# Batch 0 of a fused attention and feed-forward kernel: first loads moved to casting transfers on GpSimd, and its matmuls regrouped

## The chip, the cores and the metric

The kernel runs on one core of a Trainium2 chip. The metric is the device time of one execution in microseconds (us); lower is better. The kernel before takes 288.11 us (median of 3 runs, 288.1 to 288.44).

## The reference

```python
def _attn_ref(q_l, k_l, v_l, q_g, k_g, v_g):      # 8 batches, 8 heads, 512 local + 32 global rows, head size 64
    k_all = np.concatenate([k_g, k_l], axis=2); v_all = np.concatenate([v_g, v_l], axis=2)
    out_g = np.matmul(sm(scale * np.matmul(q_g, k_all.transpose(0, 1, 3, 2))), v_all)
    s_ll = scale * np.matmul(q_l, k_l.transpose(0, 1, 3, 2))
    s_ll = np.where(np.abs(pos[:, None] - pos[None, :]) <= 32, s_ll, -1000000000.0)
    s_lg = scale * np.matmul(q_l, k_g.transpose(0, 1, 3, 2))
    out_l = np.matmul(sm(np.concatenate([s_lg, s_ll], axis=-1)), np.concatenate([v_g, v_l], axis=2))
    return np.concatenate([out_g, out_l], axis=2)
def _moe_ref(x, w_in, w_out):                       # 4352 rows of 512; w_in 512 x 2048
    h = x @ w_in
    return (h * (1.0 / (1.0 + np.exp(-1.702 * h)))) @ w_out
```

Each of 8 batches has 8 heads. 512 local rows see a band of 64 neighbours and 32 global rows; the global rows see everything. The heads of a row are joined, and a feed-forward layer (512 to 2048, a sigmoid GELU, back to 512) follows. Inputs and output are float32; the kernel computes in bfloat16 and adds up in float32.

## The kernel before

A batch is worked as two "quads" of four heads. In batch 0 the quads are `a` (quad 0) and `c` (quad 1), objects of class `Quad`. The order of every engine's instructions is the order of the calls (a manual schedule); each engine goes through its own list in order, and semaphores join the lists. What a call does in batch 0:

- `B` writes the mask into PSUM by matmuls of an identity with a bias (TensorE, array form 128 rows by 128 columns); `S` adds the local scores (form 32 by 128); `gk` and `K` are scores against the global keys (form 32 by 32), `K` writing the bank `kb`.
- `X` and `XK` are the exponentials on ScalarE (tiles `e` and `ek`).
- `ekU` (form 32 by 32) and `U` (form 128 by 32) add up, for unit 0, the softmax sums and, for units 1 and 2, the weighted values, in banks `ov`; `Gm` (form 128 by 32) does so for the global rows, `og`.
- `R` makes reciprocals of the sums on VectorE (two transposes and a reciprocal), `XL(h)` multiplies them into the values and writes `xL`, `eg` and `G` do the global rows.
- `Tk`, `Tq`, `transpose_g` transpose keys, queries and global rows on VectorE; `ext` copies global queries beside the local ones.
- `h_mm` and `h_step` are the first feed-forward matmuls (L615), on `xL` and `w_in_sb`; kc 0 and 1 of the contraction come from quad `a`, kc 2 and 3 from quad `c`. `o_mm` (L655) is the second feed-forward layer. `fill` and `zero` are matmuls that add zero or whose result is not used.

The first loads of batch 0 go as plain float32 transfers on the ScalarE and SyncE queues (L149, L150): keys and queries of quad 0, in halves, into the tile `early`. They are cast to bfloat16 by ScalarE (`cast_act`, three times) and VectorE (L791). Global queries and keys come by SyncE (`load_g32`) and are cast by VectorE (`cast_g32`, L140). Everything else comes by casting transfers from GpSimd's queue, float32 in memory to bfloat16 on the core. Their order there is: queries, then keys of quad 1 (`load(0, (1,))`, L81 and L82), global values `rvg` (L122, L123), and in `load_rest` the values of batch 0 (L249), the 8 transfers of `w_in_sb` (L259; the mask copies L225 are put before the last two), the 4 of `w_out_sb` (L262), with batch 1's queries, keys and values among and behind them. GpSimd's transfers use eight semaphores in turn, so that each waits until the eighth before it has landed.

PSUM has four rotating one-bank tiles (`pbank`) and two two-bank tiles (`spair`); a new tile waits for the readers of the old one.

From batch 1 on, quads are objects of class `Wide`; their keys must be there before `a.S(0)` of batch 1, which stands between the `o_mm` of batch 0.

Of the kernel before, what the change touches and what calls it, by code (L numbers as in the profile page):

```python
# [12 lines left out]
F32 = mybir.dt.float32  # L13
# [7 lines left out]
def kernel(  # L21
# [53 lines left out]
    def load(b, us=(0, 1), kq=True):  # L75
        if b not in loaded:
            loaded[b] = (ld.tile([128, 2, 16 * D], BF16, name="rk"),
                         ld.tile([128, 2, 16 * D], BF16, name="rq"))
        if kq:
            s = slice(us[0], us[-1] + 1)  # L80
            nc.gpsimd.dma_start(out=loaded[b][1][:, s], in_=qf[b][:, s])  # L81
            nc.gpsimd.dma_start(out=loaded[b][0][:, s], in_=kf[b][:, s])  # L82
# [5 lines left out]
    def v_view(b, n):  # L88
        return vtiles[b % 2][:, : 8 * n * (D + 2)].rearrange("p (u j c d) -> p u j c d", u=2, j=4, c=n)
# [22 lines left out]
    def on_act(out_, in_):  # L112
        nc.scalar.activation(out_, in_, AF.Copy)  # L113
# [7 lines left out]
    def load_turned(eng, out_, in_):  # L121
        eng.dma_start(out=out_[32:128], in_=in_[0:96])  # L122
        eng.dma_start(out=out_[0:32], in_=in_[96:128])  # L123
# [7 lines left out]

    def load_g32(name, src):
        t = g32[name] = consts.tile([128, 2, D], F32, name="g32%s" % name)
        if name == "v":
            load_turned(nc.sync, t, src[:, 0:2, :])
        else:
            nc.sync.dma_start(out=t, in_=src[:, 0:2, :])

    def cast_g32(name, t):
        nc.vector.tensor_copy(t[:, 0:2, :D], g32[name])  # L140

    load(0, kq=False)
    rk, rq = loaded[0]
    early = ld.tile([128, 4, TB], F32, name="early", bufs=1)
    k32, q32 = (early[:, 2 * i : 2 * i + 2].rearrange("p a b -> p (a b)") for i in range(2))
    halves = (slice(0, 8 * D), slice(8 * D, 16 * D))
    load_g32("q", qgf)
    for f in halves:
        nc.scalar.dma_start(out=k32[:, f], in_=kf[0][:, 0, f])  # L149
        nc.sync.dma_start(out=q32[:, f], in_=qf[0][:, 0, f])  # L150
    load_g32("k", kgf)


    warm0 = consts.tile([128, 128], BF16)
    nc.gpsimd.memset(warm0, 0.0)
    step = consts.tile([128, 289], BF16)
    nc.vector.memset(step, 1.0)
    ones32 = consts.tile([128, 32], BF16)
    nc.gpsimd.memset(ones32, 1.0)
    nc.gpsimd.memset(rvg[:, :, D:], 1.0)  # L160
    bd = consts.tile([128, 4, 32], BF16)
    nc.gpsimd.memset(bd, 0.0)
    for j in range(4):
        r = (j + 1) % 4
        nc.gpsimd.memset(bd[32 * r : 32 * r + 32, j, :], 1.0)
    for i in range(2):
        vtiles.append(consts.tile([128, 8 * 5 * (D + 2)], BF16, name="v%d" % i))
        nc.gpsimd.memset(v_view(i, 4 + i)[:, :, :, :, D:], 1.0)
    nc.gpsimd.affine_select(
        out=step, in_=step, pattern=[[1, 289]], compare_op=ALU.is_ge,  # L170
        fill=0.0, base=-97, channel_multiplier=-1,
    )
    w_in_sb = wts.tile([128, 4, NKC, d_ff // 4], BF16)
    w_out_sb = wts.tile([128, FC, d_model], BF16)
    w_in_r = moe_w_in.rearrange("(u p h) f -> u p h f", u=2, h=2)
    w_out_r = moe_w_out.rearrange("(g p e) m -> p g (e m)", p=128, e=2)

    warm = consts.tile([128, 512], BF16)
    nc.vector.memset(warm, 0.0)

    def fill(n, ps, start=False):
        for _ in range(n):
            nc.tensor.matmul(ps[:, :128], lhsT=warm0, rhs=warm0, start=start, stop=start, skip_group_check=True)

    fill(21, psP.tile([128, 512], F32, name="w", tag="p"), True)

    qtiles = []
    for i in range(4):
        qt = consts.tile([128, 24, 32], F32, name="q%d" % i)
        nc.vector.memset(qt[:, 0:4, :], 0.0)  # L190
        nc.vector.memset(qt[:, 20:24, :], 0.0)
        qtiles.append(qt)

    WIN = ((0, 10), (6, 12), (14, 12), (22, 10))
    mask = consts.tile([128, 2, MW], BF16)
# [31 lines left out]
    def mask_rest():  # L227
        nc.gpsimd.memset(mask, 1.0)
        nc.gpsimd.memset(mask_at(0, 248, 16, 12)[96:128, :, 0:4], 0.0)
        nc.gpsimd.memset(mask_at(1, 236, 16, 12)[96:128, :, 8:12], 0.0)  # L230

    mask_rest()
    load(0, (1,))
    load_turned(nc.gpsimd, rvg[:, 0:2, :D], vgf[:, 0:2])

    qgT = consts.tile([128, NQ, 40], F32)
    nc.vector.memset(qgT[:, :, 32:], 0.0)
    kgT = consts.tile([128, NQ, 32], F32)
    def transpose_g(lo, hi, names="qk"):
        for name, dst, s in (("q", qgT, rqg), ("k", kgT, rkg)):  # L240
            if name not in names:
                continue
            nc.vector.transpose(dst[:, lo:hi, :32], s[:, lo:hi].bitcast(F32))
# [7 lines left out]
    def load_rest():  # L251
        load_v2(0)
        n = d_ff // 4
        for part in range(4):
            if part == 3:
                for m in MASKS:
                    make_mask(m)
            for u in range(2):
                nc.gpsimd.dma_start(out=w_in_sb[:, part, 2 * u : 2 * u + 2],  # L259
                                    in_=w_in_r[u][:, :, part * n : part * n + n])  # L260
        for g4 in (1, 0, 2, 3):
            nc.gpsimd.dma_start(  # L262
                out=w_out_sb[:, 4 * g4 : 4 * g4 + 4, :].rearrange("p (g e) m -> p g (e m)", e=2),
                in_=w_out_r[:, 2 * g4 : 2 * g4 + 2, :])
# [14 lines left out]
    def pbank(name):  # L279
        return psP.tile([128, 512], F32, name=name, tag="p")  # L280


    def spair():
        return [psS.tile([128, 2, 512], F32, name="s4", tag="s%d" % i) for i in range(2)]

    def bank(pair, j):
        return pair[j // 2][:, j % 2, :]

    class Quad:
# [29 lines left out]
            self.Tk()  # L319
            self.Tq()  # L320

        def ext(self, cs=(0, 1, 2, 3)):
            for c in cs:
                (r0, nr), t0, n = WIN[c], (0, 20, 1, 20)[c], (4, 3, 3, 4)[c]
                nc.vector.tensor_copy(
                    self.qt[:, t0 : t0 + n, r0 : r0 + nr],
                    qgT[:, self.Q, : n * nr].rearrange("p (t r) -> p t r", t=n))

# [47 lines left out]
                                     rhs=rv[:, :, ee] if len(rv.shape) == 3 else rv[:, :, :, ee],  # L376
                                     start=(ee == 0), stop=(ee == 1), skip_group_check=True)

        def X(self, rnd):
            e = self.E[rnd]  # L380
            if len(self.ps) == 4:
                for j in range(4):
                    n = RW + 32 if j == 2 else RW
                    nc.scalar.activation(e[:, j, :n], self.ps[j][:, :n], AF.Exp, scale=scale)  # L384
                return
            for i in range(2):
                nc.scalar.activation(e[:, 2 * i : 2 * i + 2, :RW], self.ps[i][:, :, :RW], AF.Exp, scale=scale)  # L387

        def K(self, e=None):
            if e != 1:  # L390
                self.kb = pbank("kb")
            self.gk(self.kb, self.q[:, 4:20], e)


        def eg(self):
# [217 lines left out]
    def h_mm(i, fc, hp, kcs):  # L613
        for kc in kcs:
            nc.tensor.matmul(hp[:, : width(i)], lhsT=w_in_c[:, fc // 4, kc, fc % 4 // 2, :, fc % 2],  # L615
                             rhs=(xL[i] if i < B else xG)[:, kc, :],
                             start=(kc == 0), stop=(kc == NKC - 1))
# [1 line left out]
    def gelu(out_, in_):  # L619
        nc.scalar.activation(out_, in_, AF.Gelu_apprx_sigmoid)  # L620

    spot = consts.tile([128, 2], F32)
    nc.gpsimd.memset(spot, 0.0)

    spot_p = consts.tile([1, 2], BF16)

    def behind(x):
# [5 lines left out]
    def exp_table():  # L633
        nc.scalar.activation(spot[:, 0:1], spot[:, 1:2], AF.Exp)
# [143 lines left out]
        for _ in range(n):  # L778
            nc.tensor.matmul(ps, lhsT=warm[:, 0:128], rhs=warm, start=False, stop=False, skip_group_check=True)

    def cast_act(r, f32, hf):
        nc.scalar.activation(r[:, 0, halves[hf]], f32[:, halves[hf]], AF.Copy)

    cast_act(rk, k32, 0)
    cast_act(rq, q32, 0)
    cast_act(rq, q32, 1)
    cast_g32("q", rqg)
    transpose_g(0, 2, "q")
    a.ext((0, 1))
    a.Tk(0, 8)  # L790
    nc.vector.tensor_copy(rk[:, 0, halves[1]], k32[:, halves[1]])  # L791
    a.Tk(8, 16)
    a.Tq(0, 8)
    a.Tq(8, 16)
    a.ext((2, 3))
    cast_g32("k", rkg)
    transpose_g(0, 2, "k")
    load_rest()
    a.B(0)
    a.B(1, split=True)  # L800
    fill(8, a.bk[1][3])
    a.S(0, added=True, part=0)
    a.S(0, added=True, part=1)
    a.X(0)
    a.S(1, split=True, added=True)
    zero(2, a.bk[1][3])
    a.X(1)
    c.Tq()
    c.ext()
    c.Tk()  # L810
    c.B(0)
    a.K()
    a.XK()
# [7 lines left out]
    pt = spair()  # L821
    c.B(1, split=True, js=(2, 3), more=[bank(pt, 0)])
    c.S(1, split=True, added=True)
    c.X(1)
    a.ekU(1)
    a.U(1)
    a.XL(0)
    c.K()
    c.XK()
    a.ekU(2, bank(pt, 2))  # L830
    a.U(2)
    a.XL(1)
    a.Gm()
    gTs[0] = moe.tile([128, FC, TB], BF16, name="gT")
    pt = spair()
    c.U(0)
    c.ekU(0)
    c.R()
    c.ekU(1)
    c.U(1)  # L840
    c.ekU(2)
    c.U(2)
    c.eg()
    for fc in range(4):
        h_mm(0, fc, bank(pt, fc), (0, 1))
    c.XL(0)
    c.XL(1)
    for kc in (2, 3):
        for fc in range(4):
            h_mm(0, fc, bank(pt, fc), (kc,))  # L850
    a.G()
    c.Gm()
    gelu(gTs[0][:, 0:2, :], pt[0])
    gelu(gTs[0][:, 2:4, :], pt[1])
    c.G()
    for fc in range(4, FC):
        h_step(0, fc)
    def osteps(i, *sts):
# [336 lines left out]
```

## Time and profile before

| | |
|---|---|
| median of 3 runs | 288.11 us |
| the profiled execution's own time | 287.94 us |
| its span | 286.0 us (1.94 us lie outside) |
| TensorE matmul busy | 280.4 us (98%) |
| VectorE, ScalarE, GpSimd busy | 205.3, 184.5, 95.3 us |
| casting transfers (queue q0, software_dynamic) | 17.83 MB, 55.9% of 16 engines |
| granted TensorE clock | 1.00 |

The span runs from the first instruction to the last. Busy time is the union of an engine's instructions. A matmul's end is modelled and includes the way through the array, so that TensorE can look busy where its starts are far apart: starts are the better guide. "Landing" is the time from a transfer's issue until its semaphore is complete.

### The profile page before, as it was taken

How to read it: one execution, taken by the hardware profiler on the slowest of the kernel's cores; microseconds unless marked ns; L12 is line 12 of the kernel's file. 1: busy time of each engine (PE TensorE's matmuls, PEld its weight loads, DVE VectorE, ACT ScalarE, POOL GpSimd, SP SyncE). 2: the span in 40 equal slices, each digit the busy share in tenths (PEclk: the TensorE clock that was granted, in tenths of full speed). 3: DMA queues.
4: the chain of work that ended last, by engine and by line, in shares of the span. 5: the costliest groups of instructions: out<-in, count | busy, mean ns of one | idle time of the engine just before them, and what ended most of it. 6: DMA issues, size and time to landing. Idle time of an engine off the chain costs nothing.

```text
span 286.0 us, 8845 instructions
## 1 busy us (share of the span) xinstructions
PE 280.4 (98%) x3727; PEld 179.5 (63%) x3727; DVE 205.3 (72%) x494; ACT 184.5 (65%) x297; POOL 95.3 (33%) x142
## 2 busy tenths in 40 slices
PE   8999999999999999999999999999999999999995
PEld 7544445544554488646884488647874589448884
DVE  7771367787689898679867998679867697363452
ACT  4847657568678784778649774877658761874331
POOL 8984550855946003920086004800040000000001
PEclk9999999999999999999999999999999999999999
DMA  7999995999999801993059803940122003200213
GB/s 203 156 191 207 203 165 79 147 224 130 155 175 187 151 3 48 94 191 60 10 88 150 147 2 77 100 66 5 28 51 73 2 3 76 73 0 2 73 35 115
DMA packets 59351, 28.23 MB, mean 99 GB/s; under 512 B 47472, under 2 KB 49776, under 8 KB 59312
## 3 DMA queue, kind: packets, MB, share of 16 engines
q0 software_dynamic: 51760, 17.83, 55.9%
q1 hardware_dynamic: 7120, 9.18, 11.5%
q8 instruction: 29, 0.48, 0.7%
q10 hardware_dynamic: 432, 0.66, 0.7%
q14 instruction: 10, 0.08, 0.1%
HBM read 36.31 MB, written 8.91 MB: 158 GB/s over the span
## 4 chain that ended last, share of the span: by engine, by line
PE 93%; DVE 2%; ACT 2%; DMA 1%; issue 0%; SPq 0%; DVEq 0%
PE hp L615 38%; PE px L726 13%; PE py L726 9%; PE op L655 9%; PE x L726 6%; PE s L560 6%; PE ov L586 5%; PE s L615 2%; DMA early<-in_q_l_dram 1%; DVE xL L471 1%; ACT e L384 1%; PE og L597 1%; PE s L356 1%; PE s L339 1%; ACT e L387 1%; DVE rs L466 1%
## 5 line engine op out<-in xcount | busy, mean ns | idle before, releaser
L615 PE MATMUL hp<-xL,w_in_sb 128*128 128x512 bf16 x480 | 105.4, 379 | 0.1
L615 PEld LDWEIGHTS <-w_in_sb 128*128 128x128 bf16 x576 | 56.1, 98 | 60.0 <-issue 0.4
L620 ACT ACTIVATE gT<-hp 128x512 bf16<-128x512 f32 x120 | 69.8, 597 | 23.9 <-PE hp L615 22.4
L571 ACT ACTIVATE e<-s 128x1016 bf16<-128x1016 f32 (+1 forms) x56 | 53.3, 1002 | 20.3 <-PE s L560 20.2
L726 PEld LDWEIGHTS <-gs 128*128 128x128 bf16 x480 | 46.2, 98 | 6.7
L699 DVE TENSOR_TENSOR gs<-gT 128x512 bf16<-128x512 bf16 (+1 forms) x90 | 30.3, 364 | 17.7 <-ACT gT L620 17.2
L576 POOL TENSOR_TENSOR e<-e,mask 128x1760 bf16<-128x1760 bf16 x4 | 13.3, 3320 | 81.1 <-ACT e L571 81.1
L98 POOL DMA_DIRECT2D v<-in_v_l_dram x40 | 31.0, 777 | 14.9 <-PE og L597 3.9
L726 PE MATMUL py<-wsum,gs 128*128 128x256 bf16 x240 | 30.3, 273 | 0.0
L655 PE MATMUL op<-w_out_sb,gT 128*128 128x512 bf16 x128 | 29.5, 380 | 0.0
L576 DVE TENSOR_TENSOR e<-e,mask 128x1712 bf16<-128x1712 bf16 (+1 forms) x24 | 25.2, 1049 | 5.6 <-ACT e L571 5.6
L512 DVE STREAM_TRANSPOSE kT<-rk 128x512 f32<-128x512 f32 x14 | 14.6, 1045 | 14.9 <-DMA rk<-in_k_l_dram 14.9
L759 POOL DMA_DIRECT2D out_dram<-ob x2 | 1.2, 598 | 69.7 <-ACT ob L113 69.5
L655 PEld LDWEIGHTS <-gT 128*128 128x128 bf16 x128 | 11.8, 98 | 13.9
L726 PEld LDWEIGHTS <-gT 128*128 128x128 bf16 x192 | 18.0, 98 | 2.7
L726 PE MATMUL px<-w_out_sb,gT 128*128 128x256 bf16 x160 | 19.2, 273 | 0.0
L726 PE MATMUL px<-w_out_sb,gs 128*128 128x256 bf16 x160 | 19.1, 273 | 0.0
L471 DVE TENSOR_TENSOR xL<-ov,rs 128x512 bf16<-128x512 f32 x27 | 17.8, 685 | 0.7 <-PE ov L438 0.2
L696 DVE TENSOR_TENSOR gs<-gT 128x1024 bf16<-128x1024 bf16 (+1 forms) x30 | 17.4, 579 | 0.0
L560 PEld LDWEIGHTS <-kT 32*128 32x128 bf16 x672 | 12.6, 93 | 7.6 <-issue 6.7
L113 ACT ACTIVATE ob<-px 128x512 f32<-128x512 f32 x10 | 6.0, 598 | 15.2 <-DVE zz L748 15.2
L560 PE MATMUL s<-q,kT 32*128 32x160 bf16 (+1 forms) x448 | 14.9, 246 | 0.0
(150 smaller groups left out, 360.3 us busy)
## 6 DMA issues: line engine op xcount, KB each, us to landing
out_dram<-ob SPq DMA_DIRECT2D x128, 64.0 KB, 3.0
rq<-in_q_l_dram POOLq DMA_DIRECT2D x5, 512.0 KB, 8.0
rk<-in_k_l_dram POOLq DMA_DIRECT2D x5, 512.0 KB, 10.0
v<-in_v_l_dram POOLq DMA_DIRECT2D x24, 96.0 KB, 4.9
w_in_sb<-in_moe_w_in_dram POOLq DMA_DIRECT2D x8, 256.0 KB, 8.3
w_out_sb<-in_moe_w_out_dram POOLq DMA_DIRECT2D x4, 512.0 KB, 10.3
rq<-in_q_l_dram POOLq DMA_DIRECT2D x5, 256.0 KB, 8.5
rk<-in_k_l_dram POOLq DMA_DIRECT2D x5, 256.0 KB, 7.9
```

Source lines behind the costliest of these rows:

```text
L98: nc.gpsimd.dma_start(out=vt[0:n, hs, c, :D], in_=vs[FIRST[c] : FIRST[c] + n, hs])
L471: nc.vector.tensor_mul(self.x[:, 2 * self.u + h, :], self.st[1 + h], self.st["rs"])
L512: nc.vector.transpose(flat[:, 0:Sl].rearrange("p (r t) -> p t r", t=16), loaded[self.b][0][:, self.u].bitcast(F32))
L560: nc.tensor.matmul(bank(self.ps, j)[:, at : at + n], lhsT=self.k[p, KEYS[c] : KEYS[c] + 128, e], rhs=qs[p, :, :, e], start=(e == 0), stop= ...
L571: nc.scalar.activation(self.E[rnd][:, 2 * i : 2 * i + 2, :n], self.ps[i][:, :, :n], AF.Exp, scale=scale)
L576: eng.tensor_mul(e, e, mask[:, rnd : rnd + 1, :n].to_broadcast([128, 4, n]))
L615: nc.tensor.matmul(hp[:, : width(i)], lhsT=w_in_c[:, fc // 4, kc, fc % 4 // 2, :, fc % 2], rhs=(xL[i] if i < B else xG)[:, kc, :], start=( ...
L620: nc.scalar.activation(out_, in_, AF.Gelu_apprx_sigmoid)
L655: nc.tensor.matmul(op, lhsT=gTs[i][:, fc, tci * 128 : tci * 128 + 128], rhs=w_out_sb[:, fc, :], start=(first and fc == 4 * f4), stop=(fc = ...
L696: nc.vector.tensor_tensor(sums[i][2][:, g, :n], t[:, g, 0, :n], t[:, g, 1, :n], ALU.add)
L699: nc.vector.tensor_tensor(sums[i][k][:, g, : n // 2], x[:, g], y[:, g], op)
L726: nc.tensor.matmul(out_, lhsT=lv[:, g, tt * 128 : tt * 128 + 128], rhs=rv[:, g, :], start=(g == 0 and k in ((1, 3, 4, 6) if self.apart els ...
```

## The change

All of it concerns batch 0 and what stands before it.

- The four halves of quad 0's keys and queries are loaded by GpSimd's casting transfers straight into `rk` and `rq`: both halves of the keys are its first two instructions, then the `affine_select` that makes `step`, then both halves of the queries. The casts on ScalarE and VectorE are gone.
- GpSimd then issues the global keys (casting), quad 1's keys, quad 1's queries (keys ahead of queries now) and only then the small fills (`ones32`, `rvg`, `v`, `bd`) with `rvg`'s loads among them. `mask_rest` moves behind six of the `w_in_sb` loads.
- The global queries still come by SyncE; their cast and the first two `ext` copies are ScalarE's, after a call that loads the exponential's table. `warm0` and `spot` are VectorE's fills; the clearing of `q` for quads 2 and 3 comes after batch 0's attention.
- In quad 1 of batch 0 VectorE does keys, `ext`, queries instead of queries, `ext`, keys.
- `fill(8)` becomes `fill(2)`. `c.K` stands right behind `c.S(1)`, into a bank of the score pair, `c.XK` between the second and third `c.X(1)`; `a.ekU(2)` stands beside `a.ekU(1)`, the three `c.ekU` stand together ahead of the three `c.U`; `c.Gm` is put between the kc 1 and kc 2 matmuls of the first `h_mm`.

```diff
     for f in halves:
-        nc.scalar.dma_start(out=k32[:, f], in_=kf[0][:, 0, f])
-        nc.sync.dma_start(out=q32[:, f], in_=qf[0][:, 0, f])
-    load_g32("k", kgf)
+        nc.gpsimd.dma_start(out=rk[:, 0, f], in_=kf[0][:, 0, f])
...
+    nc.gpsimd.affine_select(
+        out=step, in_=step, pattern=[[1, 289]], compare_op=ALU.is_ge,
+        fill=0.0, base=-97, channel_multiplier=-1,
+    )
+    for f in halves:
+        nc.gpsimd.dma_start(out=rq[:, 0, f], in_=qf[0][:, 0, f])
+    load_g(0, 2, "k")
+    nc.gpsimd.dma_start(out=rk[:, 1], in_=kf[0][:, 1])
+    nc.gpsimd.dma_start(out=rq[:, 1], in_=qf[0][:, 1])
     ones32 = consts.tile([128, 32], BF16)
     nc.gpsimd.memset(ones32, 1.0)
     nc.gpsimd.memset(rvg[:, :, D:], 1.0)
+    load_turned(nc.gpsimd, rvg[:, 0:2, :D], vgf[:, 0:2])
...
-    mask_rest()
-    load(0, (1,))
-    load_turned(nc.gpsimd, rvg[:, 0:2, :D], vgf[:, 0:2])
...
             if part == 3:
+                mask_rest()
                 for m in MASKS:
...
-    cast_act(rk, k32, 0)
-    cast_act(rq, q32, 0)
-    cast_act(rq, q32, 1)
-    cast_g32("q", rqg)
+    exp_table()
+    on_act(rqg[:, 0:2, :D], g32["q"])
     transpose_g(0, 2, "q")
-    a.ext((0, 1))
+    a.ext((0, 1), on_act)
     a.Tk(0, 8)
-    nc.vector.tensor_copy(rk[:, 0, halves[1]], k32[:, halves[1]])
     a.Tk(8, 16)
...
-    cast_g32("k", rkg)
     transpose_g(0, 2, "k")
+    nc.vector.memset(warm, 0.0)
     load_rest()
     a.B(0)
     a.B(1, split=True)
-    fill(8, a.bk[1][3])
+    fill(2, a.bk[1][3])
...
+    c.Tk()
+    c.ext()
     c.Tq()
-    c.ext()
-    c.Tk()
...
-    c.X(1)
+    c.X(1, (0, 1))
+    c.K(bank(pt, 1))
+    c.XK()
+    c.X(1, (2, 3))
     a.ekU(1)
+    a.ekU(2, bank(pt, 2))
     a.U(1)
     a.XL(0)
-    c.K()
-    c.XK()
-    a.ekU(2, bank(pt, 2))
     a.U(2)
     a.XL(1)
     a.Gm()
     gTs[0] = moe.tile([128, FC, TB], BF16, name="gT")
+    c.ekU(0)
+    c.ekU(1)
+    c.ekU(2)
     pt = spair()
     c.U(0)
-    c.ekU(0)
     c.R()
-    c.ekU(1)
     c.U(1)
-    c.ekU(2)
     c.U(2)
     c.eg()
     for fc in range(4):
         h_mm(0, fc, bank(pt, fc), (0, 1))
+    c.Gm()
...
     a.G()
-    c.Gm()
...
     c.G()
+    clear_q(2, 3)
```

More of the change, by code (lines that the diff above doesn't have):

```diff
@@ L133, in load_g32 @@
         t = g32[name] = consts.tile([128, 2, D], F32, name="g32%s" % name)
[L134 to L140, printed above, removed]
+        nc.sync.dma_start(out=t, in_=src[:, 0:2, :])
     load(0, kq=False)
@@ L144 @@
     early = ld.tile([128, 4, TB], F32, name="early", bufs=1)
-    k32, q32 = (early[:, 2 * i : 2 * i + 2].rearrange("p a b -> p (a b)") for i in range(2))
     halves = (slice(0, 8 * D), slice(8 * D, 16 * D))
@@ L148 @@
     for f in halves:
-        nc.scalar.dma_start(out=k32[:, f], in_=kf[0][:, 0, f])
-        nc.sync.dma_start(out=q32[:, f], in_=qf[0][:, 0, f])
-    load_g32("k", kgf)
+        nc.gpsimd.dma_start(out=rk[:, 0, f], in_=kf[0][:, 0, f])
     warm0 = consts.tile([128, 128], BF16)
-    nc.gpsimd.memset(warm0, 0.0)
+    nc.vector.memset(warm0, 0.0)
     step = consts.tile([128, 289], BF16)
     nc.vector.memset(step, 1.0)
+    spot = consts.tile([128, 2], F32)
+    nc.vector.memset(spot, 0.0)
+    nc.gpsimd.affine_select(
[7 more added lines that the diff above has]
+    nc.gpsimd.dma_start(out=rq[:, 1], in_=qf[0][:, 1])
     ones32 = consts.tile([128, 32], BF16)
@@ L160 @@
     nc.gpsimd.memset(rvg[:, :, D:], 1.0)
+    load_turned(nc.gpsimd, rvg[:, 0:2, :D], vgf[:, 0:2])
+    for i in range(2):
+        vtiles.append(consts.tile([128, 8 * 5 * (D + 2)], BF16, name="v%d" % i))
+        nc.gpsimd.memset(v_view(i, 4 + i)[:, :, :, :, D:], 1.0)
     bd = consts.tile([128, 4, 32], BF16)
@@ L165 @@
         nc.gpsimd.memset(bd[32 * r : 32 * r + 32, j, :], 1.0)
[L166 to L172, printed above, removed]
     w_in_sb = wts.tile([128, 4, NKC, d_ff // 4], BF16)
@@ L178 @@
     warm = consts.tile([128, 512], BF16)
-    nc.vector.memset(warm, 0.0)
     def fill(n, ps, start=False):
@@ L185, with clear_q @@
     fill(21, psP.tile([128, 512], F32, name="w", tag="p"), True)
[L187 to L192, printed above, removed]
+    qtiles = [consts.tile([128, 24, 32], F32, name="q%d" % i) for i in range(4)]
+    def clear_q(*quads):
+        for i in quads:
+            nc.vector.memset(qtiles[i][:, 0:4, :], 0.0)
+            nc.vector.memset(qtiles[i][:, 20:24, :], 0.0)
+    clear_q(0, 1)
+    qgT = consts.tile([128, NQ, 40], F32)
+    nc.vector.memset(qgT[:, :, 32:], 0.0)
+    kgT = consts.tile([128, NQ, 32], F32)
     WIN = ((0, 10), (6, 12), (14, 12), (22, 10))
@@ L230, in mask_rest @@
         nc.gpsimd.memset(mask_at(1, 236, 16, 12)[96:128, :, 8:12], 0.0)
-    mask_rest()
-    load(0, (1,))
-    load_turned(nc.gpsimd, rvg[:, 0:2, :D], vgf[:, 0:2])
-    qgT = consts.tile([128, NQ, 40], F32)
-    nc.vector.memset(qgT[:, :, 32:], 0.0)
-    kgT = consts.tile([128, NQ, 32], F32)
     def transpose_g(lo, hi, names="qk"):
@@ L320, in T, with ext @@
             self.Tq()
-        def ext(self, cs=(0, 1, 2, 3)):
+        def ext(self, cs=(0, 1, 2, 3), copy=nc.vector.tensor_copy):
             for c in cs:
                 (r0, nr), t0, n = WIN[c], (0, 20, 1, 20)[c], (4, 3, 3, 4)[c]
-                nc.vector.tensor_copy(
+                copy(
                     self.qt[:, t0 : t0 + n, r0 : r0 + nr],
@@ L377, in gk, with X @@
                                      start=(ee == 0), stop=(ee == 1), skip_group_check=True)
-        def X(self, rnd):
+        def X(self, rnd, js=range(4)):
             e = self.E[rnd]
             if len(self.ps) == 4:
-                for j in range(4):
+                for j in js:
                     n = RW + 32 if j == 2 else RW
@@ L387, in X, with K @@
                 nc.scalar.activation(e[:, 2 * i : 2 * i + 2, :RW], self.ps[i][:, :, :RW], AF.Exp, scale=scale)
[L389 to L392, printed above, removed]
+        def K(self, kb=None):
+            self.kb = pbank("kb") if kb is None else kb
+            self.gk(self.kb, self.q[:, 4:20])
         def eg(self):
@@ L620, in gelu @@
         nc.scalar.activation(out_, in_, AF.Gelu_apprx_sigmoid)
-    spot = consts.tile([128, 2], F32)
-    nc.gpsimd.memset(spot, 0.0)
     spot_p = consts.tile([1, 2], BF16)
@@ L779, in zero @@
             nc.tensor.matmul(ps, lhsT=warm[:, 0:128], rhs=warm, start=False, stop=False, skip_group_check=True)
-    def cast_act(r, f32, hf):
-        nc.scalar.activation(r[:, 0, halves[hf]], f32[:, halves[hf]], AF.Copy)
-    cast_act(rk, k32, 0)
-    cast_act(rq, q32, 0)
-    cast_act(rq, q32, 1)
-    cast_g32("q", rqg)
+    exp_table()
+    on_act(rqg[:, 0:2, :D], g32["q"])
     transpose_g(0, 2, "q")
-    a.ext((0, 1))
+    a.ext((0, 1), on_act)
     a.Tk(0, 8)
-    nc.vector.tensor_copy(rk[:, 0, halves[1]], k32[:, halves[1]])
     a.Tk(8, 16)
```

## The prediction

> **What bounds the kernel now.** The page first: TensorE is busy 98% of the span and carries 93% of the chain that ended last, so a gain must let TensorE's dense stream begin sooner. Next, the chain in order of time for 0 to 60 us (start, length, what) shows where that stream begins:
>
> ```profile
> 1.34 4.16 DMA early<-in_q_l_dram
> ...
> 5.52 1.27 ACT rq L782 x2
> ...
> 6.81 0.46 DVE q L315
> ...
> 7.31 0.47 PE s L356 x16
> 7.78 1.65 ACT e L387 x2
> ...
> 11.13 0.64 PE s L356 x16
> ...
> 13.77 1.80 ACT e L384 x4
> 15.57 0.50 ACT ek L411
> ...
> 17.89 3.56 PE s L615 x16
> ```
>
> The head is a chain: query load, two casts, transpose, scores, then ScalarE's exponentials, until the first `h_mm` at 17.82 (17.89 on the chain). From 21.7 TensorE is the chain almost alone: what `h_mm` gains is gained at the end, if later loads keep up. So I went on to the timeline and asked for single transfers with their landings:
>
> ```profile
> 5.80 1.06 PE L183 MATMUL s<-warm 128*128 128x128 bf16 x8
> 10.01 1.05 DVE L311 STREAM_TRANSPOSE kT<-rk 128x512 f32<-128x512 f32 x1 [0.48 <-DMA rk<-in_k_l_dram]
> 32.85 1.04 DVE L512 STREAM_TRANSPOSE kT<-rk 128x512 f32<-128x512 f32 x1 [10.20 <-DMA rk<-in_k_l_dram]
> 37.30 0.53 PE L560 MATMUL s<-q,kT 32*128 32x160 bf16 x16
> ...
> L81 POOL DMA_DIRECT2D rq<-in_q_l_dram x1: 552/552/552, 50.6 to 50.6; - x1
> DMA to landing us min/median/max: 4.3/4.3/4.3
> ```
>
> Quad c's scores also wait for a load (second line). Batch 1's keys land just as VectorE takes them (third), 4.45 us ahead of their matmuls (fourth). The last two lines are a 256 KB casting load with few others under way.
>
> **Part 1, quad a's loads.** Removed: the three ScalarE casts (0.63 each; 1.27 on the chain) and VectorE's (0.40 for keys, 0.23 and 0.61 for global rows). Added: casting loads on one GpSimd queue. Its issues: a 128-partition load takes 0.54 to 0.71, so two key halves from 0.81 take 1.2, the `affine_select` 0.43, two query halves 1.2: the last query half is issued at 3.04. When does it land? Rows: 128 KB stores from GpSimd at the end land 2.0 to 2.1 after issue (no other load, no cast); 256 KB loads land after 4.3 (above) and 4.7 (rq at 3.57, while the float32 loads run). In a row, loads land 1.33 apart per 256 KB (`w_in_sb`: 15.66 to 22.33 for five more) or 1.72 (rq 8.26, rk 9.98). Taking 4.3 as a fixed 3.0 and 1.3 for the data, the last half lands at 3.04 + 3.65 = 6.7; by the store rows at 5.2. I take 6.3, nearer to the loads. Then `Tq` 0.45, 0.04 to TensorE, scores 0.47: `a.X(0)` starts at 7.26 instead of 7.78, a gain of 0.5 (0.1 to 0.9). TensorE itself allows no more: `B` runs 3.50 to 5.80 from start to start, two fills follow, and the first part of `a.S(0)` needs some 0.4.
>
> The Trainium skill ("DMA: Bandwidth & Descriptors", Latency and other measured facts) puts the first byte of a transfer from GpSimd at about 1 us and from SyncE or ScalarE at about 0.6: against this change, 0.4 us per first load. The trace agrees for the loads at best (2.9 for the first float32 half), and not for the stores (2.0 to 2.1 from GpSimd, 2.2 from SyncE and ScalarE); by the page alone the gain here would be about 0.1.
>
> **Part 2, quad c's loads.** Keys are issued at 0.81 + 2.4 + 0.43 + 0.71 (global keys) = 4.35, queries at 4.95; before, queries at 3.57 and keys at 4.27. The queue then holds 0.2 of global keys and two times 1.33 to 1.72: queries land at 6.3 + 0.2 + 2.7 = 9.2 to 9.95; with part 1's bounds 8.1 to 10.3. I take 9.7; before, the last of the two landed at 9.98. What follows the late one is now `Tq` (0.71) and not `Tk` (1.05). VectorE has done keys (landed about 8.3, 1.05) and copies (0.60) by 9.95, so `c.Tq` ends at 10.66 (before 11.06), and `c.X(0)`, 0.70 behind, starts at 11.4. ScalarE would be free at 7.26 + 3.85 = 11.11 (X(0) to XK took 7.76 to 11.61), so the load decides: `c.X(0)` gains 0.42 (0.05 to 0.75) on 11.82.
>
> **Part 3, fewer stretches.** From the end of `c.S(1)` to `h_mm` (13.66 to 17.82) TensorE changes its array form eight times; now four. A `U` followed by another form takes 0.42 (16.65 to 17.07), followed by its own 0.32 (15.00 to 15.32): 0.1 a change, four saved. It also waits 0.15 for `c.XK` before `ekU`; with `c.XK` ahead of the last two exponentials that goes. At most 0.55; at least 0, if ScalarE becomes the end: X(1) and XK take 2.3 to 2.4 from there, `c.U` needs another 0.9, 3.3 in all against TensorE's 3.6 to 3.76. I take 0.4. `c.R` now begins when `c.U(0)` ends; 1.7 and `eg` and `XL(0)` (0.8) put kc 2 about 2.0 behind `h_mm`'s start, just when eight matmuls (1.73) and the moved `c.Gm` (0.3) are through. No gain or loss.
>
> **Part 4, what is pushed back on GpSimd.** All small fills now stand behind the loads: values of batch 0 are issued at 8.2 (before 6.24), `w_in_sb` at 11.5 (9.49), its last two at 19.2 (16.09, `mask_rest` 1.12 added before them). If landings moved alike, `w_in_sb` would come at 17.6 for a need at 17.0: 0.6 lost. But landings were 6 to 12 us behind issue, against 2.0 unhurried: the queue's bytes set them, and those are the same. I charge 0 (0 to 0.6). `eg`'s `bd` and `ones32` are ready at 8.2, first used at 10.9.
>
> **Part 5, later loads.** Before, batch 1's scores could start at 36.02 (last `ext`), 1.28 ahead of TensorE. With 0.8 gained 0.5 is left; if the starved queue around 8 to 9 us delays batch 1's keys by over 0.5, TensorE waits. I charge 0.05 (0 to 0.5).
>
> **Hidden:** ScalarE's table load, cast and `ext` (some 2.2 us) lie before its first exponential at 7.3; `clear_q(2, 3)` (0.6) lies in VectorE's idle 10.2 before 32.85.
>
> Sum: 0.42 + 0.4 - 0.05, about 0.75. 287.94 - 0.75 = 287.19 for an execution like the profiled one, 0.17 below the median of runs; so **287.4**.
>
> **Rivals.**
> - *One queue is too slow (slower, 0.17).* In the trace two neighbouring loads (issued 50.65 and 51.19) land at 54.97 and 57.19: 2.2 per 256 KB, with stores beside them. At that pace a's keys land at 5.1, its queries at 7.35, c's keys at 9.8, its queries at 12.0, and `c.S(0)` starts at 12.76 instead of 11.12: 1.65 lost, 0.4 regained, 289.4. It costs from c's queries landing after 10.76, over 0.2% after 11.34. For it: seven loads on one queue where two hardware queues shared the work. Against: those stores are missing here.
> - *Nothing moves (0.24).* Landings as in the rows nearest in time (4.7, then 1.72 per 256 KB): a's queries 7.2, c's 10.85, `c.S(0)` at 11.6, 0.5 lost and 0.4 regained: 288.2. The same, if loads gain 0.42 but grouping nothing (the change then doesn't do what it says): 287.7.
> - *The array clock stays low (slower, 0.04).* The eight fills start 107 ns apart for 128 columns, `h_mm`'s 217 for 512: TensorE runs at half rate until about 6.7, though the page's granted clock says 1.00. Six fills less leave it idle 0.64 more just then. If half rate lasted to `h_mm`, part 3's 3.6 would double: about 291. Against it: 0.29 idle at 9.4 in the trace did no harm. The Trainium skill ("TensorE: Matmul & The Clock Gate", What's actually happening) says that one busy window of about 3.4 us opens the gate, with a phase of its own; the trace opened it 5.6 after the first matmul.
>
> **Numbers.** The forecast has 0.53, with a range of its own from 286.8 (gains 0.75 and 0.55) to 287.7; a rest of 0.02 is late loads of part 4. About 0.2%, 0.58 us, is what a measurement of this kernel can tell from no change. Faster by more needs under 287.53: nearly all of the forecast's weight, 0.52; within 0.2% 0.26; slower 0.22. The range runs from 286.8 to 289.0, into the slow-queue case.
>
> **What would show it.** `a.X(0)` at 7.1 to 7.5 and no ACT between load and transpose; `c.Tq` ending near 10.7 and released by VectorE or a landing under 10; `h_mm` at 17.0 to 17.2; no TensorE wait for `w_in_sb`; the S of batch 1 at about 36.5. Wrong, if c's queries land after 10.8, if fills and scores keep 107 ns per 128 columns after 7 us, or if `h_mm` starts early and TensorE waits at batch 1's scores.

## The result and the profile after

The changed kernel takes 290.75 us (median of 4 runs, 290.26 to 291.31) against 288.11: 1.0086 times the kernel before, 95% interval 1.0069 to 1.0102. It is slower, and the forecast was faster. The profiled execution took 290.69, with a span of 288.7 against 286.0.

The page's first line and its chain by engine, after. TensorE's share of the chain was 93% before; it lost ten points, mostly to GpSimd and transfers:

```profile
span 288.7 us, 8829 instructions
...
PE 83%; DMA 7%; POOL 5%; DVE 3%; issue 1%; ACT 0%; POOLq 0%; DVEq 0%
```

The chain in order of time, after (start, length, what). Where the kernel before had one load and then ScalarE and TensorE, a load of quad c's queries now ends at 12.95, then GpSimd's issues and batch 1's keys lead up to batch 1's scores:

```profile
1.34 1.25 POOL rk L142 x2
...
5.38 7.57 DMA rq<-in_q_l_dram
...
13.23 3.51 POOL w_in_sb L255 x5
...
23.51 13.01 DMA rk<-in_k_l_dram
...
39.73 0.64 PE s L555 x23
```

The timeline after, asked engine by engine (start, length, engine, what; in brackets the idle time before it and what ended it):

```profile
1.34 1.25 POOL L142 DMA_DIRECT2D rk<-in_k_l_dram  x2 [0.82 <-POOLq L1167]
...
6.30 0.30 PE L180 MATMUL s<-warm 128*128 128x128 bf16 x2
7.54 0.43 PE L352 MATMUL s<-q,kT 32*128 32x120 bf16 x16 [0.94 <-DVE q L311]
8.59 0.94 PE L352 MATMUL s<-q,kT 32*128 32x80 bf16 x32 [0.62 <-DVE q L311]
...
9.05 1.66 ACT L383 ACTIVATE e<-s 128x856 bf16<-128x856 f32 x2 [4.56 <-PE s L352]
...
11.49 1.04 DVE L307 STREAM_TRANSPOSE kT<-rk 128x512 f32<-128x512 f32 x1 [2.36 <-DMA rk<-in_k_l_dram]
12.97 0.71 DVE L311 STREAM_TRANSPOSE q<-rq 128x512 f32<-128x512 f32 x1 [0.18 <-DMA rq<-in_q_l_dram]
...
13.74 0.67 PE L352 MATMUL s<-q,kT 32*128 32x200 bf16 x16 [0.33 <-DVE q L311]
...
36.54 1.04 DVE L507 STREAM_TRANSPOSE kT<-rk 128x512 f32<-128x512 f32 x1 [12.01 <-DMA rk<-in_k_l_dram]
39.73 0.53 PE L555 MATMUL s<-q,kT 32*128 32x160 bf16 x16 [0.29 <-ACT q L113]
```

Behind the two fills that are left TensorE waits twice for the halves of quad a's queries, `a.X(0)` starts at 9.05 instead of 7.76 (7.78 in the chain), quad c's keys come at 11.47 instead of 9.99, its queries at 12.95 instead of 8.26, and batch 1's scores now wait 0.29 where they waited for nothing. The timeline before, for quad c's queries, `c.S(0)` and `h_mm`:

```profile
8.29 0.71 DVE L315 STREAM_TRANSPOSE q<-rq 128x512 f32<-128x512 f32 x1
...
11.12 0.66 PE L356 MATMUL s<-q,kT 32*128 32x200 bf16 x16
...
17.82 2.55 PE L615 MATMUL s<-xL,w_in_sb 128*128 128x512 bf16 x11
```

The stages between 6 and 13 us, after (window; length of the window, then busy time and count of TensorE, its weight loads, VectorE, ScalarE and GpSimd; then granted clock, DMA share, GB/s):

```profile
6.00:8.00 2.00, 1.03 (x22) 0.73 (x21) 0.45 (x1) 0.00 (x0) 1.88 (x9) 1.00 1.09 108
8.00:9.00 1.00, 0.41 (x24) 0.39 (x24) 0.90 (x5) 0.00 (x0) 0.93 (x3) 1.00 1.03 150
9.00:10.00 1.00, 1.00 (x29) 0.51 (x19) 0.14 (x3) 0.95 (x2) 1.00 (x3) 0.88 1.07 170
10.00:11.00 1.00, 1.00 (x7) 0.58 (x6) 0.00 (x0) 1.00 (x2) 1.00 (x2) 0.50 1.64 167
11.00:12.00 1.00, 1.00 (x10) 0.57 (x11) 0.51 (x1) 1.00 (x4) 0.79 (x2) 0.50 1.95 148
12.00:13.00 1.00, 1.00 (x10) 0.27 (x3) 0.82 (x6) 0.57 (x2) 0.47 (x1) 0.50 2.20 139
```

One of these stages before:

```profile
10.00:11.00 1.00, 1.00 (x14) 0.41 (x12) 0.99 (x2) 1.00 (x4) 0.94 (x3) 1.00 2.38 139
```

From 10 us on TensorE's granted clock is half after, and full before. So there are two suspects for quad c's late start, its load and the clock, and they lie in the same microseconds.

**How batch 0 adds up.** Four starts in each trace split the time: `a.X(0)`; from it to `c.S(0)`; from there to `h_mm`; from there to batch 1's first scores ("S1").

| kernel | `a.X(0)` | to `c.S(0)` | to `h_mm` | to S1 | lowest clock, 8 to 17 us | ratio to before (95%) |
|---|---|---|---|---|---|---|
| before | 7.76 | 3.36 | 6.70 | 19.48 | 1.00 | |
| after | 9.05 | 4.69 | 6.14 | 19.85 | 0.50 | 1.0086 (1.0069 to 1.0102) |
| e1, e12 regrouping alone | 7.80, 8.31 | 3.31, 3.31 | 6.14, 6.15 | 19.49, 19.48 | 1.00 | 0.9985 (0.9975 to 0.9996), 0.9968 (0.9956 to 0.998) |
| e2 loads alone | 9.00 | 4.06 | 6.71 | 19.48 | 1.00 | 1.0105 (1.0068 to 1.0142) |
| e3 longer fills | 9.02 | 4.24 | 6.15 | 19.88 | 1.00 | 1.0091 (1.0075 to 1.0106) |
| e4 masks later | 8.78 | 4.63 | 6.15 | 19.65 | 1.00 | 1.0069 (1.0057 to 1.0081) |
| e5 float32 loads for a | 10.27 | 5.38 | 6.57 | 19.48 | 0.50 | 1.0101 (1.008 to 1.0122) |
| e6 fills on VectorE | 9.09 | 4.16 | 6.14 | 19.69 | 1.00 | 1.0065 (1.0044 to 1.0086) |
| e7 global keys by SyncE | 9.17 | 4.22 | 6.15 | 19.49 | 0.50 | 1.0082 (1.006 to 1.0104) |
| e8 a's keys float32 | 8.17 | 3.31 | 6.14 | 19.61 | 1.00 | 0.9986 (0.9976 to 0.9997) |
| e9 e7 and e3 | 9.16 | 3.31 | 6.37 | 19.26 | 1.00 | 1.0047 (1.003 to 1.0063) |
| e10 e9, e4 and e6 | 9.26 | 3.31 | 6.38 | 19.26 | 1.00 | 1.004 (1.0021 to 1.0059) |
| e11 e10, a's queries float32 | 8.08 | 3.31 | 6.15 | 19.51 | 1.00 | 0.9995 (0.9984 to 1.0006) |

The times and the clock are from one profiled execution each; the ratio is from all runs, each against runs of the kernel before made beside it. For the change, `h_mm` is later by 1.29 + 1.33 - 0.56 = 2.06 (19.88 against 17.82), S1 by 0.37 more, and the end by 0.3 beyond that.

### The profile page after: what moved, and what is told of

The parts are those of the page before. It is cut to its first block, busy times and chain, and to the rows that moved or that the text cites. A ratio compares the mean times of both kernels' runs of the same rounds, so it can differ in the third digit from the quotient of the medians.

```text
span 288.7 us, 8829 instructions
## 1 busy us (share of the span) xinstructions
PE 280.5 (97%) x3721; PEld 179.4 (62%) x3721; DVE 203.2 (70%) x491; ACT 183.6 (64%) x298; POOL 97.8 (34%) x145
## 4 chain that ended last, share of the span: by engine, by line
PE 83%; DMA 7%; POOL 5%; DVE 3%; issue 1%; ACT 0%; POOLq 0%; DVEq 0%
PE hp L610 34%; PE px L718 13%; PE py L718 9%; PE op L647 7%; PE x L718 6%; PE s L555 6%; PE ov L581 5%; DMA rk<-in_k_l_dram 5%; DMA rq<-in_q_l_dram 3%; POOL w_in_sb L255 2%; PE s L610 1%; POOL mask L227 1%; DVE xL L466 1%; PE og L592 1%; DVE rs L461 0%
```

## The experiments

**e1, e12: the regrouping alone.** The kernel before with the new order of TensorE's work from `c.X(1)` on; its loads untouched.

```diff
-    c.X(1)
+    c.X(1, (0, 1))
+    c.K(bank(pt, 1))
+    c.XK()
+    c.X(1, (2, 3))
...
+    c.Gm()
     c.XL(0)
```

> All loads, casts, fills and masks as before; only the regrouping of batch 0's matmuls as changed (c.K behind c.S(1) in a score bank, c.XK between the c.X(1) halves, a.ekU(2) beside a.ekU(1), the three c.ekU together, c.Gm between kc 1 and kc 2). Late queue (the casting loads on one GpSimd queue land later and carry the whole loss): this is 0.2 to 0.5 us faster than before, 287.6 to 287.9, with h_mm at 17.3 to 17.6 instead of 17.82. Regrouping (the new order of matmuls itself costs): 288.7 or more. Low clock (TensorE's half rate carries the loss): like before or faster, since here TensorE has no longer waits for loads.

> The kernel of e1 (the kernel before with the regrouping alone) once more, beside e11 on the same chip. In e1 it took 287.5, with an interval that ended at 0.9996. Theory: the regrouping is worth 0.45 to 0.6; again 0.9975 to 0.9995 times the kernel before, h at 17.2 to 17.4. Rival: e1 was a lucky draw of the load landings; then 1.000 within 0.001.

Measured: 287.5 and, on another chip, 287.62 (before there: 288.38). Both intervals lie under 1; e12 gained more than the 0.9975 to 0.9995 that I expected. In the timeline of e1:

```profile
17.25 1.90 PE L614 MATMUL s<-xL,w_in_sb 128*128 128x512 bf16 x8
```

against 17.82 before; `c.S(0)` is at 11.11 against 11.12. The profiled execution of e12 drew late loads (the last query half at 6.68, 6.12 before; `a.X(0)` at 8.31, `h_mm` at 17.77), but the stretch from `c.S(0)` to `h_mm` is 6.15 in it too. In every kernel with the old order (before, e2) this stretch is 6.70 or 6.71, in the others at full clock 6.14 or 6.15, save for e9 and e10 (in both, `h_mm` waits 0.16 for VectorE's `sT`). The regrouping is worth 0.56, and alone it is faster than both kernels.

**e2: the loads alone.** The changed kernel with the old order of matmuls from `c.X(1)` on (the diff of e1 backwards).

> The complement: casting loads on GpSimd, order of loads, casts, fills and masks as changed; the matmuls of batch 0 in the order of before, except that c still does keys, ext, queries. Late queue: 290.9 to 291.3, the changed kernel's 290.75 plus what the regrouping saves (0.2 to 0.5), c's queries landing near 12.95 as in the changed kernel. Regrouping: 288 to 289.5. Low clock: near 290.75.

Measured: 290.55; the runs spread from 289.52 to 293.49, so the loads cost 2.0 to 4.1 by its interval. The time lies under the 290.9 to 291.3 of the late queue and near the figure of the low clock, so it cannot choose between them; the trace can. `h_mm` in e2:

```profile
19.77 0.61 PE L611 MATMUL s<-xL,w_in_sb 128*128 128x512 bf16 x2
```

The granted clock is 1.00 in every stage up to there: in this execution the loads make `h_mm` 1.95 later without any low clock. The clock was not always so: three of e2's six executions have a mean clock of 0.997 to 0.999 and took 289.52 to 290.24, the other three 0.993 or 0.994 and took 290.86 to 293.49. A half-clock stretch like the change's (3.4 us, see the last section) lowers the mean by 0.006.

**e3: the clock kept up.** Idle TensorE is filled with matmuls that add zero.

```diff
-    fill(2, a.bk[1][3])
+    fill(20, a.bk[1][3])
     a.S(0, added=True, part=0)
+    fill(12, a.bk[1][3])
```

> The changed kernel with fill(20) instead of fill(2) before a.S(0) and fill(12) between its two parts, so that TensorE has work while the queries are under way (idle from about 6.5 to 7.5 and 8.0 to 8.6 in the changed kernel). Low clock: the granted clock stays 1.00 from 9 to 13 us (0.50 in the changed kernel) and the time falls by 1 us or more, to 289.7 or less. Late queue: the clock may stay high, but c.S(0) still waits for c's queries (13.0), so the time moves by 0.3 us at most.

Measured: 290.63, no better. The same window as above, in e3:

```profile
10.00:11.00 1.00, 0.58 (x7) 0.44 (x6) 0.00 (x0) 1.00 (x3) 1.00 (x2) 1.00 1.27 126
```

The clock is full, TensorE idles instead, and `c.S(0)` waits for the load (queries at 12.47). `h_mm` came at 19.41, 0.47 before the change's. But the chain of e3 reaches S1 over batch 1's keys, which landed at 36.08 (36.52 in the change), so that S1 could not follow at the distance of 19.48 that it has before:

```profile
24.00 12.08 DMA rk<-in_k_l_dram
...
39.29 0.64 PE s L555 x23
```

**e4: the mask work behind the last two `w_in_sb` loads.**

```diff
-            if part == 3:
-                mask_rest()
-                for m in MASKS:
-                    make_mask(m)
...
+        mask_rest()
+        for m in MASKS:
+            make_mask(m)
```

> The changed kernel with GpSimd's mask fills and mask copies (3.5 us) moved behind the last two w_in_sb loads, so that these are issued at about 16.7 instead of 20.2; w_out_sb's issue stays where it was. Starved queue (the DMA engines run out of work from 20 to 24 us, 157 GB/s instead of 200, while GpSimd makes masks, so that batch 1's keys land at 36.5 and TensorE waits 0.3 there): batch 1's keys land 0.5 to 0.9 earlier, TensorE does not wait for a.S(0) of batch 1, 0.3 to 0.5 us faster, 290.3 to 290.5. Late queue alone: 290.75 within 0.2, for h_mm starts at 19.9 as before this edit.

Measured: 290.17, a little under my 290.3 to 290.5. Batch 1's keys landed at 35.39 instead of 36.52, and S1 came 0.2 sooner behind `h_mm`. The interval overlaps that of the change.

**e5: quad a's loads and the global keys as before, all else as changed.**

```diff
-        nc.gpsimd.dma_start(out=rk[:, 0, f], in_=kf[0][:, 0, f])
+        nc.scalar.dma_start(out=k32[:, f], in_=kf[0][:, 0, f])
+        nc.sync.dma_start(out=q32[:, f], in_=qf[0][:, 0, f])
+    load_g32("k", kgf)
```

> The changed kernel, but quad a's keys and queries and the global keys come again as float32 transfers on ScalarE's and SyncE's queues and are cast as before; GpSimd begins with the affine_select and then quad c's keys and queries, all else as changed. Late queue (what stands ahead of them in the one queue delays c's loads): c's queries land at 8 to 9.5 instead of 12.95, a.X(0) starts at 7.8 to 8.3, and the time is at or below the regrouping alone, 287.2 to 287.9. If instead the fills behind the loads or the order keys, queries carried the loss: 289 or more.

Measured: 291.23 (the profiled execution, 292.64, is its longest run), no gain at all; I had expected 287.2 to 287.9. With quad a off GpSimd's queue, quad c's loads went out at 1.78 and 2.48 and competed: the second query half landed at 8.52 (6.12 before), the global keys at 10.97 (6.33), quad c's queries at 10.67. The timeline of e5:

```profile
11.00 0.23 DVE L788 CAST rkg<-g32k 128x128 bf16<-128x128 f32 x1 [1.19 <-DMA g32k<-in_k_g_dram]
...
15.65 0.90 PE L352 MATMUL s<-q,kT 32*128 32x200 bf16 x16
```

TensorE ran at half clock from 7.2 to 17.4 in this execution, and the mean clock of all five (0.982 to 0.988) is low, so that the start at 15.65 and the time are not due to the loads alone. The landings do show the loads at work: the early issue of quad c's loads costs quad a what its own queues gave it. So the streams of different queues hold each other up. The Trainium skill ("DMA: Bandwidth & Descriptors", Issuing engines are not separate DMA queues) says that transfers of all issuing engines run on the same 16 and interleave, and the trace agrees.

**e6: GpSimd's small fills on VectorE** (`ones32`, `rvg`, `v`, `bd`: `nc.gpsimd.memset` becomes `nc.vector.memset`).

> The changed kernel with the small fills that stand between quad c's loads and the values' loads on GpSimd (ones32, rvg, v, bd) made by VectorE before it would wait. Disturbed queue (GpSimd's fills at 5.9 to 8.2 slow the transfers under way; packets of quad c's keys take up to 1.08 us there): c's queries land before 11.5 instead of 12.95 and the time falls by 1 us or more. Late queue: c's queries land at 12.5 to 13; only the values come 1 us sooner, and the time falls by 0 to 0.4.

Measured: 290.04. The second quad's queries landed at 12.43, half a microsecond earlier than in the change and as in e2 to e4 (12.27 to 12.62), which left these fills alone: the fills are not what holds the queue up.

**e7: the global keys by SyncE,** as float32 with a cast on VectorE, instead of on GpSimd's queue between quad a and quad c.

```diff
     load_g32("q", qgf)
+    load_g32("k", kgf)
...
-    load_g(0, 2, "k")
...
+    nc.vector.tensor_copy(rkg[:, 0:2, :D], g32["k"])
```

> The changed kernel with the global keys as a float32 transfer on SyncE's queue and a cast on VectorE (as before) instead of a casting transfer of 128-byte packets between quad a's queries and quad c's keys. Small packets (those 256 packets hold up quad c's loads): c's queries land 1 us or more earlier, near 11.5, and the time falls by 1 us. Late queue by bytes: 0.2 to 0.8 earlier (one issue of 0.7 less), time 0.2 to 0.8 lower, 290.0 to 290.5.

Measured: 290.77. Quad c's queries land at 10.87, 2.1 earlier, as the case of the small packets had it, but the time stays, where that case had 1 us less. Timeline, then windows, of e7:

```profile
10.90 0.71 DVE L311 STREAM_TRANSPOSE q<-rq 128x512 f32<-128x512 f32 x1
...
13.39 0.67 PE L352 MATMUL s<-q,kT 32*128 32x200 bf16 x16
```

```profile
6.00:8.00 2.00, 0.63 (x14) 0.46 (x16) 0.54 (x2) 0.00 (x0) 1.81 (x9) 1.00 1.16 190
...
10.00:11.00 1.00, 1.00 (x5) 0.47 (x4) 1.00 (x6) 1.00 (x3) 1.00 (x2) 0.50 2.10 139
```

The queries are transposed by 11.61, and their scores begin 1.78 later: TensorE, at half clock, is still at the work ahead of them. Between 6 and 8 us the transfers move 190 GB/s here and 108 in the change.

**e8: a split,** on top of the regrouping: quad a's keys as float32 by ScalarE and SyncE, its queries first on GpSimd's queue, quad c's loads next, the mask work as in e4.

```diff
-        nc.scalar.dma_start(out=k32[:, f], in_=kf[0][:, 0, f])
-        nc.sync.dma_start(out=q32[:, f], in_=qf[0][:, 0, f])
+        (nc.scalar if f is halves[0] else nc.sync).dma_start(out=k32[:, f], in_=kf[0][:, 0, f])
+        nc.gpsimd.dma_start(out=rq[:, 0, f], in_=qf[0][:, 0, f])
...
-    cast_act(rq, q32, 0)
-    cast_act(rq, q32, 1)
```

> The regrouped matmuls of e1, with quad a's first loads split: keys as float32 halves, one on ScalarE's and one on SyncE's queue, with casts as before; queries as casting transfers, the first two of GpSimd, without ScalarE's casts; then affine_select, quad c's loads, the small fills, the rest, masks behind the last w_in_sb load. Late queue: queries land at 5.2 to 6.2, a.X(0) starts at 6.9 to 7.4 (7.8 in e1), c's loads land at 8.5 to 9.5, time 286.9 to 287.6, at or below e1. If one queue less is enough to delay: a.X(0) later than 7.8 and more than 287.7.

Measured: 287.81, as e1, not better. The query halves, GpSimd's first two instructions, landed at 6.10 and 7.06, 4.8 and 5.0 behind their issue, and `a.X(0)` began at 8.17, where I had expected 6.9 to 7.4: no sooner than with two float32 loads and two casts (7.76 before, 7.80 in e1, 8.31 in e12). That is the rival's case.

**e9: e7 and e3 together.**

> The changed kernel with two edits together: the global keys come over SyncE as f32 with a cast (as in e7), and the longer fills of e3 (20 ahead of a's first scores, 12 between the parts). Alone they moved the time to 290.77 and 290.63, against 290.75 for the change. Theory: two limits stand near one another in batch 0, the late second quad's queries (12.95 in the change) and the array's half clock between 10 and 13 us; taking away one leaves the other. Then both together give a granted clock of 1.00, the second quad's queries at about 10.9, its first scores at 11.7 to 11.9, batch 0's output matmul h at 17.9 to 18.2 instead of 19.88, and, with batch 1 then held by its keys, 288.4 to 289.3. Rival: one of the two counts for nothing and the loss is somewhere further on; then 290.3 to 290.8 again.

Measured: 1.0047 of before (median 290.12, 288.95 to 290.4). I had expected 288.4 to 289.3. The profiled execution is the shortest, 1.2 under the median, so what the others lose besides is not seen. In it, from `a.X(0)` to `c.S(0)` it takes 3.31, as in e1: that excess, 1.33 against before, is gone with both causes taken away, and was cut only to 4.22 and 4.24 with one. My numbers for `c.S(0)` and `h_mm` were missed (12.47, not 11.9; 18.84, not 18.2): I had forgotten that `a.X(0)` was itself 1.4 late. The chain of e9:

```profile
4.00 2.50 PE s L335 x16
6.51 1.12 PE s L180 x20
...
9.18 1.65 ACT e L383 x2
10.83 0.04 issue
10.87 0.63 PE s L335 x6
11.50 0.56 PE kb L371 x8
12.06 0.48 PE s L335 x4
12.54 0.60 PE s L352 x16
```

From the exponentials on there is no load and no gap in it. Up to them it runs over the added fills, so these have a part in the late `a.X(0)`.

**e10: e9 with e4 and e6.**

> e9 with the two edits on the later loads added: the mask work behind the last two input weight loads (e4) and the small fills of ones, values and block diagonals on VectorE (e6). Theory: with batch 0 mended, what is left is batch 1's keys, whose landing these two edits bring forward (e4 by 1.1 us, e6 by 0.7); the time comes to 287.8 to 288.5, that is to the kernel before or a little below it. Rival: the later loads are hidden; then this is e9 within 0.2 us. If the cause lies outside the loads and the clock, 289.5 or above.

Measured: 1.004 of before (median 289.28); its interval overlaps e9's. Its batch 0 is e9's, and so is its distance to S1. With batch 0 as late as it is here, mending the later loads shows no further gain; the forecast for it was missed. In its profiled execution (289.76) S1 is at 38.21, 0.11 behind e9's, and the span ends 1.03 behind: some 0.9 is lost behind S1, for a reason that stays open.

**e11: e10 with quad a's queries by the float32 queues,** cast on ScalarE, its keys still on GpSimd's queue.

```diff
+    for f, eng in zip(halves, (nc.sync, nc.scalar)):
+        eng.dma_start(out=q32[:, f], in_=qf[0][:, 0, f])
     load_g32("q", qgf)
...
-    for f in halves:
-        nc.gpsimd.dma_start(out=rq[:, 0, f], in_=qf[0][:, 0, f])
...
-    fill(20, a.bk[1][3])
+    fill(8, a.bk[1][3])
...
-    fill(12, a.bk[1][3])
```

> e10 with the first quad's queries taken off GpSimd's queue again: two float32 halves at the head of SyncE's and ScalarE's queues, both cast on ScalarE, its keys still casting loads on GpSimd; the fills are 8 and 0 instead of 20 and 12. In e10 the second quad's queries landed at 10.75, and its first scores still began only at 12.57, because the first quad's exponentials began at 9.28 (7.78 in the kernel before). Theory: what is left of the loss in e10 (h at 18.95 against 17.82) is the first quad's query halves behind its keys and the affine_select on GpSimd's queue (7.87 in e10). Then the halves land by 4.6, the exponentials begin at 6.9 to 7.4, the second quad's first scores at 10.3 to 11.0, h at 16.7 to 17.4, and the time is 286.8 to 287.8, a little below the kernel before. Rival: the two kinds of queue hold each other up as in e5; then the halves or the keys land after 6.5, the exponentials begin at 8 or later and the time is 288.5 or above. Third: with fewer fills the granted clock falls to 0.50 again, h at 19 or later.

Measured: 0.9995 of before (288.37), so the loss is gone; the gain hoped for is not there. The regrouping alone took 287.62 on the same chip (e12), so these loads still cost about 0.75. The query halves landed at 4.00 and 4.18 as expected, but the key halves at 5.77 and 6.67 (5.52 for the later one in e10), as the rival had it. The chain of e11:

```profile
2.04 4.63 DMA rk<-in_k_l_dram
...
6.70 0.61 DVE kT L307
...
7.36 0.74 PE s L352 x25
8.10 1.65 ACT e L383 x2
```

The last half to land, now one of the keys, sets `a.X(0)` again. Against e10 some 0.4 of the gain is due to the fills: there the second part of the scores stood behind the twelve (queries transposed by 8.34, scores at 8.80).

## Why the prediction was wrong, step by step

- **Part 1, quad a's loads** (gain 0.5 forecast, 1.29 lost): the term that failed is the landing of the last query half, "I take 6.3". It was 8.07, and the rest of the sum held: transpose, scores and `a.X(0)` follow within 0.98 (0.96 forecast). GpSimd's first transfer began at 1.34, not 0.81 (SyncE's began at 0.82 in the same trace), so the half was issued at 3.60 instead of 3.04; and it took 4.47 to land, where I had taken 3.26. I had split the 4.3 of a 256 KB load into a fixed 3.0 and 1.3 for data, and halved the second. The transfers' landings, after:

```profile
L155 POOL DMA_DIRECT2D rq<-in_q_l_dram x2: 560/568/576, 3.0 to 3.6; - x2
L158 POOL DMA_DIRECT2D rq<-in_q_l_dram x1: 571/571/571, 5.4 to 5.4; - x1
...
DMA to landing us min/median/max: 4.0/4.5/7.6
```

  A half (first line, 3.97 and 4.47) takes nearly as long as the whole 256 KB did before (4.3, 4.7). My bound of 6.7 was short as well. Before, the chain went on from the first query half, landed at 5.50, since the second landed at 6.12, while ScalarE cast the first. So the load that starts it is 2.57 later, the two casts saved are 1.27, and the difference of 1.30 is the loss. That the queries' place in the queue carries about 1.0 of the loss is shown by e11, where `a.X(0)` is back at 8.08 (e11 differs in other edits too).
- **Part 2, quad c's loads** (gain 0.42 forecast): quad c's queries landed 3.25 behind my 9.7. Of this 1.77 is part 1's error, handed on, and the other 1.48 belongs to this part: "0.2 of global keys" was the second mis-sized term. With them out of the queue (e7, e9) quad c's keys come 1.34 and 1.48 behind quad a's last half, and its queries 1.34 and 1.35 after them: the 1.33 to 1.72 of the prediction. With them in the queue quad c's keys came 3.21 behind the global keys' landing at 8.26. Taking them out brought quad c's queries forward by 2.1; at most 0.75 of that is the issue taken off GpSimd, and how the rest splits between the transfer's packets and what they do to the next one was not tried.
- **Part 3, fewer stretches** (0.4, at most 0.55): right, 0.56 (e1, e12, and by e2 in reverse). How it splits between the saved changes of form and the wait of 0.15 was not tried.
- **Part 4, what is pushed back on GpSimd** (0): the weights were in time; no TensorE wait for `w_in_sb` appears. **Part 5, later loads** (0.05, up to 0.5): 0.37 between `h_mm` and S1 in the profile after, with 0.29 of it the wait shown above. The chain after shows the link: GpSimd's issues stand behind the landing of quad c's queries at 12.95, and batch 1's keys behind these issues. So that late load delays S1 a second time; in e7, where it landed at 10.87, the keys landed at 34.26 and S1 followed `h_mm` by 19.49. That moving the masks (e4) recovers a measurable part of the time is not shown.
- **The rivals.** "One queue is too slow" came nearest: it had quad c's queries at 12.0 and `c.S(0)` at 12.76; 12.95 and 13.74 came, and 290.75 instead of its 289.4. Late landings were right, but that the numbers are near is partly luck. It gave all loads one pace of 2.2 per 256 KB; measured were 2.74 from quad a's keys to its queries, 3.40 to quad c's keys and 1.48 to its queries. A late start, a long landing and one small transfer did it. "The array clock stays low" happened too, from 10 to 13 us, and not by missing the first opening but by closing again. It is not what makes the change slow: of the change's four executions three have a mean clock of 0.993 or 0.994, and the fourth, at 0.998, took 290.80, in the midst of their 290.26 to 291.31. e3, at full clock, was no faster either, and the profiled executions of e2, e4 and e6 were slow without it. What it costs on top is open: in e2 the executions with the lower clock were the longer ones, in e4 they were the shortest and the longest. With the load mended and the clock not, it took the load's place in the trace of e7, and with both mended the excess is gone in that of e9. By their times e9 (1.0030 to 1.0063) is clear of e3 (1.0075 to 1.0106), but not of e7 (1.0060 to 1.0104), whose one execution at 0.998 took 290.63, as long as the rest.
- **The chances.** I gave 0.22 to slower; no case had quad a's queries later than 7.35. All cases let GpSimd's first load begin at 0.81 and took their landings from rows of 256 KB loads, and so shared their errors. The first sign of being wrong that the prediction names, c's queries landing after 10.8, is the one that came.

## What to carry to other kernels

When first loads change queues, cost them by when their issue begins and by the landing of a whole transfer behind it; halving a transfer here did not halve its landing. Work that needs four loads is set by the one that lands last: compare the landing that starts the chain, old and new (5.50 and 8.07), before counting saved casts (1.27). Where two edits each move little, look whether the two waits they remove lie in the same microseconds, and remove both (e3, e7, e9); and split the path into stretches, so that a gain (6.70 to 6.14) can be seen under a larger loss.

## What the runs showed of the hardware

- The granted clock of the change fell to 0.50 between 9 and 10 us (0.88 in that window), after TensorE had been busy 1.03 of 2.00 us (6 to 8) and 0.41 of 1.00 (8 to 9), with no single wait over 0.94. The Trainium skill ("TensorE: Matmul & The Clock Gate", What's actually happening) closes the gate after an idle window of about 3.4 us. The trace does not show a window of that length without work: TensorE was idle 1.6 of those 3 us.
- The clock records kept with the traces tell more. Full clock begins at 6.35 in the change and ends 3.41 later; half clock then lasts 3.41, and three times that in e5. TensorE's busy time in the first 3.41 of full clock was 1.85 in the change, 1.66 in e7 and 1.25 in e5, where the clock then fell, and 2.05 (e11) to 3.41 (e3) in the eleven other profiled executions, where it did not. In these traces the limit lies between 1.85 and 2.05 of 3.41; no run was made to test it. Of the two rows at the limit the first is the change's, the second e11's:

```profile
6.35:9.76 3.41, 1.85 (x61) 1.19 (x59) 1.48 (x6) 0.71 (x1) 3.23 (x11) 1.00 1.06 128
...
4.41:7.82 3.41, 2.05 (x55) 1.88 (x56) 2.56 (x8) 1.42 (x5) 3.41 (x6) 1.00 1.15 193
```

- Full clock begins anywhere from 3.77 to 7.25, and differs for one and the same kernel (4.36 in e1, 5.39 in e12). The mean clocks of one kernel's executions differ too (e2, above). So whether the clock falls is, as far as these runs show, in part drawn anew in each execution. In e2, with the change's loads, full clock began at 6.85 and its 3.41 held 2.14 of work; there it stayed.
- The first transfer from GpSimd started at 1.34 or 1.35 in every kernel whose GpSimd list began with one, 0.5 after SyncE's; a fill there started at 0.81 before.
- A casting load's landing was 3.2 to 3.6 for the two key halves where these were GpSimd's first, with only global rows beside them on other queues; 4.4 and 4.6 for the same halves with float32 queries beside them (e11); and 3.7 to 5.0 for query halves with others beside them. The Trainium skill ("DMA: Bandwidth & Descriptors", Anatomy of one DMA) gives 2.0 us and the bytes at 436 GB/s, an estimate of 2.3 for 128 KB. No half here came that fast.
